# The left-over rows of the last four output tiles in one 64-row stretch at the end of a gated attention and MLP kernel

## The chip, the cores and the metric

The kernel runs on one core of one Trainium2 chip. The metric is device time in microseconds (us). A core has a matmul engine (TensorE; PE in the profile, PEld its weight loads), a vector engine (DVE), an activation engine (ACT), a general one (POOL) and SyncE (SP), from whose queue most transfers are issued. A finished tile is evicted, that is scaled and copied out of TensorE's accumulators by ACT or DVE, and then stored by a transfer to memory; a store lands when the signal of its completion arrives.

A ratio compares two kernels that ran in the same rounds, with a 95% interval; it is not quite the ratio of the medians quoted beside it. A "gain" without a view named is always a difference of such times; positions inside a run come from the trace of one profiled execution.

## The reference, cut to what matters

```python
x = A_x                                            # 2048 x 512
g = sigmoid((x * gate_w).sum(-1, keepdims=True))
a = attention(x, ...)                              # o @ wo, o: 2048 x 512
b = einsum('bsf,fd->bsd', z1 * (w_sp @ z2 + b_sp), w_out)   # u = z1 * (...): 2048 x 688
return g * a + (1 - g) * b
```

The output has 16 tiles of 128 rows. A tile is `oT.T @ wo + uT.T @ w_out`, scaled: four matmuls of 128 contraction rows for the attention part, and 688 = 5 * 128 + 48 rows for u. These 48 left-over rows are what the change is about.

## The kernel before

u of a tile is kept in 768 columns, padded with 80 zeros, and is transposed in six blocks of 128 rows. In even tiles the 48 left-over rows are the first ones of block 5 (in partitions 0 to 63, the lower half), in odd tiles the last ones of block 0 (in partitions 64 to 127, the upper half). So the left-over matmul of an even and of an odd tile each use one half of TensorE's rows, and can run side by side. The weights `w_rem` hold both halves, with zeros between, so a matmul over all 128 rows gives the same result.

```python
def ba_spat(acc, tt, start, c0=0, c1=D):          # five matmuls of 128 rows
    ...
def ba_rem(acc, tt, rows, stop, c0=0, c1=D):      # the 48 left-over rows
    nc.tensor.matmul(
        acc, lhsT=uTs[tt][rows, 5 * (1 - tt % 2), :], rhs=w_rem[rows, c0:c1], start=False, stop=stop)

def ba_tile(tt, cuts=(0, D)):                     # tiles 14 and 15
    for h, (c0, c1) in enumerate(zip(cuts, cuts[1:])):
        acc = acc_tile()[:, 0:c1 - c0]
        ba_spat(acc, tt, True, c0, c1)
        ba_rem(acc, tt, slice(0, P), False, c0, c1)       # all 128 rows
        ba_attn(acc, tt, False, True, c0, c1)
        ba_store(acc, tt, c0, c1, h > 0)                  # second piece: DVE and SP, else ACT

def ba_step(tt):                                  # tiles 0 to 13
    group = next(g for g in BA_GROUPS if tt in g)
    accs[tt] = acc_tile()
    ba_attn(accs[tt][:, :], tt, True, False)
    ba_spat(accs[tt][:, :], tt, False)
    if tt == group[-1]:
        for t in group:
            ba_rem(accs[t][:, :], t, halves[t % 2], True)  # 64 rows each, side by side
        if tt + 2 < NT - 1:
            attn_tile_64(tt + 2)                           # more 64-row work
        for t in group:
            ba_store(accs[t][:, :], t, 0, D, False)        # ACT evicts and issues

BA_GROUPS = [range(0, 4), range(4, 8), range(8, 12), range(12, 14)]
...
    ba_tile(14)
    ba_tile(15, cuts=(0, 384, D))
```

The softmax here doesn't subtract the row's maximum and nothing guards it: scores larger than these inputs give would overflow.

## Time and profile before

| | before |
|---|---|
| median, 3 runs (range) | 207.25 us (206.95 to 207.43) |
| span of the profiled run | 205.4 us |
| PE busy, of the span | 201.2 us, 98% |
| chain that ended last, on PE | 96% |

The first two lines are from the page of the kernel before: busy time of each engine with its share of the span and its instructions, and the chain that ended last by engine. The chain is followed back from the last instruction to what released each step.

```profile
PE 201.2 (98%) x1564; PEld 120.3 (59%) x1564; DVE 129.8 (63%) x282; ACT 75.4 (37%) x123; POOL 46.4 (23%) x77
...
PE 96%; DMA 2%; ACTq 0%; DVE 0%; issue 0%
```

TensorE is the bound nearly everywhere. So time is to be saved by taking work from TensorE, or behind its last matmul.

Next comes the chain of the kernel before in order of time, near its end. The columns are start and length in us, then engine, output and line. L520 is the spatial part (`uT.T @ w_out`), L514 the attention part, L524 the left-over rows.

```profile
196.69 1.08 PE mm L520 x5
197.77 0.32 PE mm L524 x2
198.09 1.19 PE mm L520 x5
199.28 0.22 PE mm L524
199.50 0.86 PE mm L514 x4
200.36 0.81 PE mm L520 x5
201.17 0.16 PE mm L524
201.33 0.65 PE mm L514 x4
201.98 0.28 PE mm L520 x5
202.26 0.06 PE mm L524
202.32 0.24 PE mm L514 x4
```

The chain gives prices directly. Five spatial matmuls of 512 columns take 1.08, so one takes 0.22. A left-over matmul over 128 rows costs the same as any other of its width: 0.22 for tile 14, 0.16 and 0.06 for the two pieces of tile 15. The 64-row pair of tiles 12 and 13 takes 0.32 for both, and the five spatial matmuls behind it take 1.19 instead of 1.08. The earlier stretches of four take 0.54, so one more pair adds 0.22. So the pair itself costs 0.22, and by difference entering the 64-row form costs about 0.10 and leaving it 0.11.

Behind the last matmul lies a tail. These are the timeline's lines of the kernel before for the two pieces of tile 15: start, length, engine, line, operation. ACTq and SPq are the issues of the two stores.

```profile
202.02 0.58 ACT L535 ACTIVATE ob<-mm,g_inv 128x384 bf16<-128x384 f32 x1 [0.89 <-PE mm L514]
202.58 0.35 DVE L531 TENSOR_SCALAR ob<-mm,g_inv 128x128 bf16<-128x128 f32 x1 [5.34 <-PE mm L514]
202.63 0.34 ACTq L536 DMA_DIRECT2D out_dram<-ob  x1
202.96 0.38 SPq L533 DMA_DIRECT2D out_dram<-ob  x1
```

The first piece is evicted by ACT and stored from its queue, the second by DVE and stored from SP. The trace has the landings at 204.28 and 204.46, and the program ends at 205.38.

### The profile page before, as it was taken

How to read it: one execution, taken by the hardware profiler on the slowest of the kernel's cores; microseconds unless marked ns; L12 is line 12 of the kernel's file. 1: busy time of each engine (PE TensorE's matmuls, PEld its weight loads, DVE VectorE, ACT ScalarE, POOL GpSimd, SP SyncE). 2: the span in 40 equal slices, each digit the busy share in tenths (PEclk: the TensorE clock that was granted, in tenths of full speed). 3: DMA queues.
4: the chain of work that ended last, by engine and by line, in shares of the span. 5: the costliest groups of instructions: out<-in, count | busy, mean ns of one | idle time of the engine just before them, and what ended most of it. 6: DMA issues, size and time to landing. Idle time of an engine off the chain costs nothing.

```text
span 205.4 us, 4012 instructions
## 1 busy us (share of the span) xinstructions
PE 201.2 (98%) x1564; PEld 120.3 (59%) x1564; DVE 129.8 (63%) x282; ACT 75.4 (37%) x123; POOL 46.4 (23%) x77
## 2 busy tenths in 40 slices
PE   8999999999999999999999999999999999999994
PEld 4566666655665555656565666555555555665642
DVE  4377575747977687979797788555566645633330
ACT  3466577796222233332424042222251136002222
POOL 5020202020522425334242442222204220200000
PEclk9999999999999999999999999999999999999999
DMA  6998599999999017940433229763566568552942
GB/s 175 265 183 186 92 212 209 206 259 206 265 245 217 3 38 158 307 91 13 83 29 63 51 38 117 143 117 71 100 161 51 119 114 181 67 97 55 145 89 78
DMA packets 90100, 27.22 MB, mean 133 GB/s; under 512 B 84225, under 2 KB 90081, under 8 KB 90081
## 3 DMA queue, kind: packets, MB, share of 16 engines
q1 hardware_dynamic: 87312, 24.55, 64.1%
q10 hardware_dynamic: 2736, 2.42, 4.3%
q8 instruction: 12, 0.20, 0.4%
q14 instruction: 8, 0.06, 0.1%
q0 software_dynamic: 32, 0.00, 0.0%
HBM read 4.15 MB, written 2.10 MB: 30 GB/s over the span
## 4 chain that ended last, share of the span: by engine, by line
PE 96%; DMA 2%; ACTq 0%; DVE 0%; issue 0%
PE mm L459 36%; PE zp L192 18%; PE mm L360 14%; PE mm L520 8%; PE mm L514 7%; PE mm L400 7%; DMA w_z<-in_B_w_in_dram 2%; PE kvacc L416 2%; PE at L472 2%; PE mm L524 1%; PE zp L312 0%; PE at L483 0%; PE zp L231 0%; ACTq L118 0%; ACTq L121 0%; PE pq L312 0%
## 5 line engine op out<-in xcount | busy, mean ns | idle before, releaser
L459 PE MATMUL mm<-z2all,wspT 128*128 128x344 bf16 x512 | 79.9, 309 | 0.0
L459 PEld LDWEIGHTS <-wspT 128*128 128x128 bf16 x512 | 49.0, 98 | 25.3
L192 PE MATMUL zp<-w_z,xT 128*128 128x344 bf16 x252 | 37.9, 309 | 0.1
L364 ACT ACTIVATE eq<-mm 128x512 bf16<-128x512 f32 x32 | 17.4, 594 | 51.4 <-PE mm L360 25.7
L368 DVE TENSOR_REDUCE zs<-eq 128x64 f32<-128x1024 bf16 x16 | 19.5, 1220 | 20.1 <-ACT eq L364 20.1
L192 PEld LDWEIGHTS <-xT 128*128 128x128 bf16 x252 | 24.3, 98 | 12.0 <-DVE xT L291 0.3
L364 ACT ACTIVATE ek<-mm 128x512 bf16<-128x512 f32 x32 | 17.3, 601 | 27.1 <-PE mm L360 27.1
L377 POOL TENSOR_TENSOR eq<-eq,ratio 128x512 bf16<-128x512 bf16 x16 | 16.9, 1056 | 44.6 <-DVE ratio L376 36.7
L464 DVE SCALAR_TENSOR_TENSOR ucat<-mm,bT,z1all 128x344 bf16<-128x344 f32 x32 | 17.4, 544 | 14.9 <-PE mm L459 14.9
L535 ACT ACTIVATE ob<-mm,g_inv 128x512 bf16<-128x512 f32 (+1 forms) x16 | 10.9, 680 | 32.4 <-PE mm L524 26.6
L368 DVE TENSOR_REDUCE zs<-ek 128x64 f32<-128x1024 bf16 x16 | 19.3, 1209 | 2.8 <-ACT ek L364 2.8
L520 PE MATMUL mm<-wspT,uT 128*128 128x512 bf16 (+2 forms) x85 | 20.1, 367 | 0.0
L360 PEld LDWEIGHTS <-xT 128*128 128x128 bf16 x128 | 12.2, 98 | 12.0
L377 POOL TENSOR_TENSOR ek<-ek,ratio 128x512 bf16<-128x512 bf16 x16 | 16.9, 1056 | 2.2 <-DVE ratio L376 1.7
L514 PE MATMUL mm<-wspT,oT 128*128 128x512 bf16 (+2 forms) x68 | 16.6, 366 | 0.0
L360 PE MATMUL mm<-wq_p,xT 128*128 128x512 bf16 x64 | 16.4, 379 | 0.0
L400 PE MATMUL mm<-wv_sb,xT 128*128 128x512 bf16 x64 | 16.4, 379 | 0.0
L360 PE MATMUL mm<-wk_p,xT 128*128 128x512 bf16 x64 | 16.3, 379 | 0.0
L210 DVE BATCH_NORM_STATS2 bn<-z2all 128x6 f32<-128x344 bf16 x32 | 14.9, 503 | 0.0
L207 ACT ACTIVATE z2all<-zp 128x688 bf16<-128x688 f32 x16 | 11.8, 743 | 7.8 <-PE zp L192 7.7
L265 ACT ACTIVATE z1all<-zp 128x688 bf16<-128x688 f32 x16 | 11.9, 743 | 5.1 <-PE zp L192 4.7
L520 PEld LDWEIGHTS <-uT 128*128 128x128 bf16 x85 | 8.1, 98 | 9.4 <-issue 0.2
(78 smaller groups left out, 145.3 us busy)
## 6 DMA issues: line engine op xcount, KB each, us to landing
out_dram<-ob ACTq DMA_DIRECT2D x15, 128.0 KB, 2.2
wspT<-in_B_w_out_dram SPq DMA_DIRECT2D x2, 640.0 KB, 5.0
w_z<-in_B_w_in_dram SPq DMA_DIRECT2D x2, 344.0 KB, 4.8
wv_sb<-in_A_wqkv_dram SPq DMA_DIRECT2D x2, 256.0 KB, 3.6
wspT<-in_A_wo_dram SPq DMA_DIRECT2D x2, 256.0 KB, 4.0
w_z<-in_B_w_in_dram SPq DMA_DIRECT2D x2, 172.0 KB, 4.2
xs<-in_A_x_dram SPq DMA_DIRECT2D x2, 128.0 KB, 2.7
uT<-ucat SPq DMA_TRANSPOSE x16, 2.8
```

What stands on the lines that cost most here:

```text
L192: nc.tensor.matmul(zp[:, j, 0:n], lhsT=xT[:, dt, tt * P:(tt + 1) * P], rhs=wt[:, dt, j * HF:j * HF + n], start=(dt == first), stop=(dt == ...
L210: nc.vector.bn_stats(out=bn6[:, tt, j, :], in_=z2v[:, j, :])
L265: nc.scalar.activation(out=z1all[:, tt, :].rearrange("p (j n) -> p j n", j=2), in_=zp[:, :, 0:HF], func=AF.Gelu_apprx_tanh,)
L360: nc.tensor.matmul(ps[:, :], lhsT=xT[:, dt, tt * P:(tt + 1) * P], rhs=w[:, dt, :], start=(dt == 0), stop=(dt == NDT - 1))
L364: nc.scalar.activation(out=e[:, :, a, :], in_=ps[:, :].rearrange("p (h f) -> p h f", f=DH), func=AF.Exp, scale=1.0 - 2.0 * a)
L368: nc.vector.tensor_reduce(out=z[:].rearrange("p h a -> p (h a)"), in_=e[:].rearrange("p h a f -> p (h a) f"), axis=AX.X, op=ALU.add,)
L377: nc.gpsimd.tensor_tensor(out=e[:, :, 1, :], in0=e[:, :, 1, :], in1=ratio[:, :, None].to_broadcast([P, H, DH]), op=ALU.mult)
L400: nc.tensor.matmul(v_ps[:, :], lhsT=xT[:, dt, tt * P:(tt + 1) * P], rhs=wv_sb[:, dt, :], start=(dt == 0), stop=(dt == NDT - 1))
L459: nc.tensor.matmul(gp[:, 0:HF], lhsT=wspT[:, st, tt * P:(tt + 1) * P], rhs=z2all[:, st, j * HF:(j + 1) * HF], start=(st == 0), stop=(st == ...
L464: nc.vector.scalar_tensor_tensor(out=ucat[tt % NU][:, c0 + j * HF:c0 + (j + 1) * HF], in0=gp[:, 0:HF], scalar=bT[:, tt:tt + 1], in1=z1all[ ...
L514: nc.tensor.matmul(acc, lhsT=oTs[tt][:, g, :], rhs=wo_t[:, g, c0:c1], start=start and g == 0, stop=stop and g == NG - 1)
L520: nc.tensor.matmul(acc, lhsT=uTs[tt][:, i + ft, :], rhs=w_main[i][:, ft, c0:c1], start=start and ft == 0, stop=False)
```

## The change

Its intent: tile 14's left-over matmul (lower half) should run beside those of tile 15's two pieces (upper half), in the 64-row stretch that tiles 12 and 13 pay for anyway. As tiles 12 to 14 are then evicted late, DVE takes one of them, and SP issues all three stores so that ACT is free for tile 15. The core of the diff:

```diff
-    def ba_rem(acc, tt, rows, stop, c0=0, c1=D):
+    def ba_rem(acc, tt, start=False, c0=0, c1=D):
+        rows = halves[tt % 2]
         nc.tensor.matmul(
-            acc, lhsT=uTs[tt][rows, 5 * (1 - tt % 2), :], rhs=w_rem[rows, c0:c1], start=False, stop=stop)
+            acc, lhsT=uTs[tt][rows, 5 * (1 - tt % 2), :], rhs=w_rem[rows, c0:c1], start=start, stop=not start)
 ...
-            nc.scalar.dma_start(out=dst, in_=ob[:, :])
+            (nc.sync if on_sp else nc.scalar).dma_start(out=dst, in_=ob[:, :])
 ...
-    def ba_tile(tt, cuts=(0, D)):
 ...
+    def ba_last():
+        last = NT - 1
+        ba_step(last - 1)
+        pieces = [(acc_tile()[:, 0:384], 0, 384), (bank_tile(q_bank)[:, 0:P], 384, D)]
+        for t in BA_GROUPS[-1][:-1]:
+            ba_rem(accs[t][:, :], t)
+        for acc, c0, c1 in pieces:
+            ba_rem(acc, last, True, c0, c1)
+        for n, t in enumerate(BA_GROUPS[-1][:-1]):
+            ba_store(accs[t][:, :], t, on_dve=n == 1, on_sp=True)
+        for n, (acc, c0, c1) in enumerate(pieces):
+            ba_spat(acc, last, False, c0, c1)
+            ba_attn(acc, last, False, True, c0, c1)
+            ba_store(acc, last, c0, c1, on_dve=n == 1)
 ...
-    BA_GROUPS = [range(0, 4), range(4, 8), range(8, 12), range(12, 14)]
+    BA_GROUPS = [range(0, 4), range(4, 8), range(8, 12), range(12, 16)]
 ...
-        ba_tile(14)
-        ba_tile(15, cuts=(0, 384, D))
+        ba_last()
```

More of the change, by code (lines that the diff above doesn't have):

```diff
@@ L521, in ba_spat, with ba_store @@
                              start=start and ft == 0, stop=False)
-    def ba_rem(acc, tt, rows, stop, c0=0, c1=D):
+    def ba_rem(acc, tt, start=False, c0=0, c1=D):
+        rows = halves[tt % 2]
         nc.tensor.matmul(
-            acc, lhsT=uTs[tt][rows, 5 * (1 - tt % 2), :], rhs=w_rem[rows, c0:c1], start=False, stop=stop)
-    def ba_store(acc, tt, c0, c1, on_dve):
+            acc, lhsT=uTs[tt][rows, 5 * (1 - tt % 2), :], rhs=w_rem[rows, c0:c1], start=start, stop=not start)
+    def ba_store(acc, tt, c0=0, c1=D, on_dve=False, on_sp=False):
         ob = work.tile([P, c1 - c0], BF16, name=f"ob{c1 - c0}", bufs=4 if c1 - c0 == D else 1)
@@ L540, in acc_tile @@
         return bank_tile(acc_banks[-1])
-    def ba_tile(tt, cuts=(0, D)):
-        for h, (c0, c1) in enumerate(zip(cuts, cuts[1:])):
-            acc = acc_tile()[:, 0:c1 - c0]
-            ba_spat(acc, tt, True, c0, c1)
-            ba_rem(acc, tt, slice(0, P), False, c0, c1)
-            ba_attn(acc, tt, False, True, c0, c1)
-            ba_store(acc, tt, c0, c1, h > 0)
+    def ba_last():
[12 more added lines that the diff above has]
+            ba_store(acc, last, c0, c1, on_dve=n == 1)
     def ba_step(tt):
@@ L556, in ba_step @@
             for t in group:
-                ba_rem(accs[t][:, :], t, halves[t % 2], True)
-            if tt + 2 < NT - 1:
-                attn_tile_64(tt + 2)
+                ba_rem(accs[t][:, :], t)
+            attn_tile_64(tt + 2)
             for t in group:
-                ba_store(accs[t][:, :], t, 0, D, False)
+                ba_store(accs[t][:, :], t)
     oTs = {}
```

## The prediction

> **What bounds the kernel now.** TensorE. The page's busy table gives PE 201.2 us of a span of 205.4 us (98%) at a full granted clock, and the chain that ended last is PE for 96%. So the change is worth what it takes from TensorE's last 5 us, plus or minus what it does to the tail behind it.
>
> **What the change does to TensorE.** Matmul counts and weight loads stay (3130 PE rows in both, the same up to tile 13's spatial matmuls). In the chain of waits, in time order from 197.77 us (end of tile 13's spatial part), before has: 64-row pair of tiles 12 and 13 0.32, tile 14 1.19 + 0.22 + 0.86, first piece of 15 0.81 + 0.16 + 0.65, second piece 0.28 + 0.06 + 0.24, end at 202.56. Costs to read from it:
> - 128-row left-over matmuls: 0.22 (512 columns), 0.16 (384), 0.06 (128), together 0.44 us;
> - the 64-row pair costs 0.22 for both, as they run side by side, plus about 0.10 on entry (0.32 less 0.22) and 0.11 on leaving (the next five spatial matmuls take 1.19 instead of 1.08). The Trainium skill ("TensorEngine Tiling (Array Packing)", Key Properties) says changing the tiling mode drains TensorE and that different tiles run in parallel; this trace agrees with both. The stretch of four at 187.87 takes 0.54, one more pair for 0.22.
>
> After, the stretch holds tiles 12, 13, 14 and both pieces of 15. Tile 14 (lower rows, 512 columns) runs beside 384 + 128 columns of tile 15 (upper rows), so it should cost 0.54. Entry and exit stay one each. Estimate from these durations: 0.86 + 1.08 (tile 14), 0.54, then 0.92 + 0.65 and 0.28 + 0.24 = 4.57, so the last matmul ends near 202.34 instead of 202.56: 0.22 us less, all on the chain.
>
> **Inputs in time?** Tile 14 now starts with attention, needed at 197.6; its transposed o landed near 195.6. Tile 15's transposed u landed near 199.0 and is now needed near 199.9, not 200.2. Its o landed near 200.0, needed near 201.0. Slack about 0.9 us; no new wait.
>
> **Stores.** Tiles 12, 13 and 14 are evacuated only after the stretch, near 200.05: 12 and 14 on ACT (0.69 each), 13 on DVE (128 columns take 0.35; estimate for 512 about 0.75), all three issued from SP (0.38 each), done by about 202.0. All are free for the pieces, at 201.8 and 202.35. The stores start about 0.4 us apart and should land by 203.5 (1.7 us each before). The last DVE eviction, issue and landing (0.35 + 1.5 us) then keep their length and shift by 0.22 us.
>
> **Predicted time:** 207.25 - 0.22 = 207.0 us, range 206.75 to 207.3 (before: 206.95 to 207.43). Chances: faster by over 2% 0.01, within 2% 0.98, slower 0.01.
>
> **What would show it right.** The chain has one 64-row group of five of about 0.54 us, no 128-row left-over matmul, and the last matmul ends about 0.22 us earlier; the last store is issued about 0.22 us earlier with the same 1.5 us to landing.
>
> **What would make it wrong.** A PE wait for tile 15's u before the stretch; the two pieces of 15 not running beside tile 14 (stretch 0.7 or more); an ACT, DVE or SP still busy with tiles 12 to 14 when tile 15's pieces end; the three bunched stores delaying the last landing.

## The result, and the profile after

| | before | after |
|---|---|---|
| median, 6 runs each (range) | 207.34 us (206.93 to 207.74) | 207.05 us (206.99 to 207.24) |
| ratio | 1 | 0.999, 95% interval 0.9975 to 1.0005 |
| span of the profiled run | 205.4 us | 205.3 us |

The times alone cannot tell the change from nothing: the interval contains 1. The trace can. This is the chain after, from the same point (the end of tile 13's spatial part); L525 is the left-over rows, L532 the last eviction.

```profile
196.80 1.08 PE mm L520 x5
197.88 0.86 PE mm L514 x4
198.74 1.08 PE mm L520 x5
199.82 0.54 PE mm L525 x4
200.36 0.92 PE mm L520 x5
201.28 0.65 PE mm L514 x4
201.93 0.28 PE mm L520 x5
202.21 0.24 PE mm L514 x4
202.44 0.02 issue
202.47 0.35 DVE ob L532
```

The three left-over matmuls on 128 rows are gone, and one stretch of 0.54 holds all five (the chain counts four; one that runs beside another is not a link of it). From the end of tile 13's spatial part to the end of the last matmul it is 202.44 - 197.88 = 4.56 us; before it was 202.56 - 197.77 = 4.79. (The chain follows the last matmul to its signal, 0.01 to 0.02 later than the matmul's own end, which the table below uses.)

The timeline's lines of the tail after, beginning with the last of the three stores that SP issues for tiles 12 to 14:

```profile
201.83 0.40 SPq L537 DMA_DIRECT2D out_dram<-ob  x1
201.96 0.58 ACT L536 ACTIVATE ob<-mm,g_inv 128x384 bf16<-128x384 f32 x1 [0.52 <-PE mm L514]
202.47 0.35 DVE L532 TENSOR_SCALAR ob<-mm,g_inv 128x128 bf16<-128x128 f32 x1 [1.45 <-PE mm L514]
202.57 0.34 ACTq L537 DMA_DIRECT2D out_dram<-ob  x1
202.85 0.33 SPq L534 DMA_DIRECT2D out_dram<-ob  x1
```

All engines are free in time for tile 15. But the two last issues are now 0.27 us apart (before 0.33), and the last store took 1.57 us to land (before 1.50). So of TensorE's 0.22 us, about 0.15 reach the last landing.

Why the times are so blurred can also be read from the traces. In every trace whose kernel is unchanged up to there, 150.84 to 150.87 us pass from the first matmul with `w_sp` (L459, which makes u) to the end of tile 13's spatial part. That first matmul itself, however, starts anywhere from 46.43 to 47.32 us; in all but one (e2) the difference is already there at 9 us, among the first loads and matmuls. These 0.9 us are about as wide as the spread of the times, several times the effect, and come before anything that the change touches. So the experiments are read in two ways: by their times where some tenths of a per cent are expected, and else by distances inside a trace, from the end of tile 13's spatial part.

This table is worked out from the traces, in us, in the order: end of tile 13's spatial part to the last matmul's own end; distance of the two last store issues; time to landing of the first and of the second piece of tile 15; end of tile 13's spatial part to the last landing. The labels are those of the experiments below.

```
                     to last matmul  issues apart  first lands  second lands  to last landing
before                   4.770          0.329         1.650        1.499          6.688
after                    4.553          0.271         1.669        1.565          6.535
e8 (after again)         4.553          0.273         1.656        1.550          6.521
e1 (order)               4.557          0.272         1.656        1.550          6.524
e9 (order, widths)       4.557          0.272         1.669        1.564          6.539
e2 (two stretches)       4.768          0.272         1.654        1.549          6.734
e3 (all on 128 rows)     4.773          0.272         1.667        1.561          6.751
e5 (15 on 128 rows)      4.767          0.328         1.653        1.491          6.675
e4 (all on ACT)          4.552       first is last    1.628        1.487          7.953
e6 (two issues on ACT)   4.553       first is last    1.628        1.506          6.798
e7 (cut at 416)          4.553          0.092         1.740        1.814          6.751
e10 (cut at 368)         4.554          0.362         1.661        1.505          6.493
e11 (cut at 352)         4.553          0.450         1.650        1.513          6.516
```

### The profile page after: what moved, and what is told of

The parts are those of the page before. It is cut to its first block, busy times and chain, and to the rows that moved or that the text cites. A ratio compares the mean times of both kernels' runs of the same rounds, so it can differ in the third digit from the quotient of the medians.

```text
span 205.3 us, 4014 instructions
## 1 busy us (share of the span) xinstructions
PE 201.2 (98%) x1564; PEld 120.2 (59%) x1564; DVE 130.5 (64%) x283; ACT 74.6 (36%) x122; POOL 46.4 (23%) x77
## 4 chain that ended last, share of the span: by engine, by line
PE 95%; DMA 2%; ACTq 0%; DVE 0%; issue 0%
PE mm L459 36%; PE zp L192 18%; PE mm L360 14%; PE mm L520 8%; PE mm L514 7%; PE mm L400 7%; DMA w_z<-in_B_w_in_dram 2%; PE kvacc L416 2%; PE at L472 2%; PE mm L525 1%; PE zp L312 0%; PE at L483 0%; PE zp L231 0%; ACTq L118 0%; ACTq L121 0%; PE pq L312 0%
## 5 line engine op out<-in xcount | busy, mean ns | idle before, releaser
L459 PE MATMUL mm<-z2all,wspT 128*128 128x344 bf16 x512 | 79.9, 309 | 0.0
L459 PEld LDWEIGHTS <-wspT 128*128 128x128 bf16 x512 | 49.0, 98 | 25.3
L536 ACT ACTIVATE ob<-mm,g_inv 128x512 bf16<-128x512 f32 (+1 forms) x15 | 10.1, 680 | 33.1 <-PE mm L525 28.5
```

The lines of the kernel that those rows point to most:

```text
L459: nc.tensor.matmul(gp[:, 0:HF], lhsT=wspT[:, st, tt * P:(tt + 1) * P], rhs=z2all[:, st, j * HF:(j + 1) * HF], start=(st == 0), stop=(st == ...
```

## The experiments

The theory: tile 14's left-over matmul takes no time of its own because it runs beside those of tile 15, and this is the whole gain on TensorE. Rivals: a 64-row matmul is cheaper as such; one stretch instead of several forms saves the switch; the moved evictions and stores are the gain. All kernels below are edits of the changed kernel, and all gave correct results.

### e5_last_full: tile 14 in the stretch, tile 15 not

```diff
-        for acc, c0, c1 in pieces:
-            ba_rem(acc, last, True, c0, c1)
 ...
-            ba_spat(acc, last, False, c0, c1)
+            ba_spat(acc, last, True, c0, c1)
+            nc.tensor.matmul(acc, lhsT=uTs[last][:, 0, :], rhs=w_rem[:, c0:c1], start=False, stop=False)
```

> The changed kernel's stores and one stretch, but only tiles 12, 13 and 14 in it; the two pieces of 15 take their left-over rows on all 128 rows, as before. Theory (pairing 14 with 15 is the whole gain): 14 stands alone in its turn, so tile 13's spatial end to the last matmul's end is 4.79 us as before, ratio to before 1.000. Rival (moved stores, or tile 14 as 64 rows, are the gain): 4.6 us or less, or a span as short as the changed kernel's.

Ratio to before 0.9999 (0.9982 to 1.0017), median 207.1 beside 207.18. The chain of this run, with L553 the left-over rows of tile 15 on 128 rows:

```profile
199.88 0.53 PE mm L525 x3
200.41 0.92 PE mm L520 x5
201.33 0.16 PE mm L553
...
202.42 0.06 PE mm L553
```

The stretch with three matmuls takes 0.53, no less than the one with five after the change (0.54), and the 0.16 and 0.06 of tile 15 are back on top. To the last matmul it is 4.77 us, as before. A 64-row matmul alone is therefore not cheaper, and stores and evictions moved as in the change bring nothing to TensorE. The gain is the pairing.

### e2_two_stretches: the pairing kept, the one stretch undone

```diff
-    BA_GROUPS = [range(0, 4), range(4, 8), range(8, 12), range(12, 16)]
+    BA_GROUPS = [range(0, 4), range(4, 8), range(8, 12), range(12, 14), range(14, 16)]
 ...
-            attn_tile_64(tt + 2)
+            if tt + 2 < NT - 1:
+                attn_tile_64(tt + 2)
 ...
-            ba_store(accs[t][:, :], t, on_dve=n == 1, on_sp=True)
+            ba_store(accs[t][:, :], t)
```

> Tiles 12 and 13 have their own 64-row stretch with stores on ACT as before; 14 and the two pieces of 15 share a second one. The pairing of 14 with 15 is kept, and one more entry and exit is paid. Theory (pairing is worth 0.22, one entry and exit 0.10 + 0.11): from tile 13's spatial end to the last matmul's end 4.76 us, within 0.03 of before's 4.79; so no gain without the one stretch. Rival (the switch costs nothing once the pipe is full): 4.56 us, as the changed kernel. Ratio to before 0.999 to 1.000.

Ratio 1.001 (0.9989 to 1.003), median 207.29 beside 207.03. Its chain:

```profile
197.91 0.32 PE mm L525 x2
198.23 0.97 PE mm L514 x4
199.20 1.08 PE mm L520 x5
200.28 0.33 PE mm L525 x2
200.61 0.92 PE mm L520 x5
```

Both pairs cost 0.32 to 0.33, and behind both the next group is longer by 0.11 (0.97 for 0.86, 0.92 for 0.81). The second entry and exit eat the 0.22 that the pairing saves: 4.77 us to the last matmul. Collecting all five in one stretch is a needed half of the change.

### e3_full_rows: every pairing undone

```diff
-        rows = halves[tt % 2]
+        rows = slice(0, P)
```

> The changed kernel with all 17 left-over matmuls on all 128 rows (same result, the other rows meet zeros): every pairing is undone, in the three earlier groups too. Theory (each pair hides 0.216 us, all of it on the chain): each earlier group's four take about 0.43 us more (two pairs), 1.30 in all; the last group is as in the kernel before. So 1.3 us longer than before, ratio 1.006. Rival (TensorE's spare time hides it, or the 64-row form and the switches eat what pairing gives): ratio 1.000 to 1.002.

Median 208.68 beside 207.03, ratio 1.0079 (1.0059 to 1.0099), so slower clear of noise; the mean is longer by 1.6 us, with an interval of about 1.2 to 2.0, so 1.3 is inside it. The left-over group of the third of the earlier stretches and the attention matmuls behind it, in the chain of the kernel before and then in the chain of this run (the groups of the other two stretches take 0.54 and 0.86 as well):

```profile
187.87 0.54 PE mm L524 x4
188.41 0.19 PE at L483 x16
```

```profile
188.88 0.86 PE mm L525 x4
189.75 0.30 PE at L483 x16
```

Four matmuls take 0.86 instead of 0.54, and the entry into the 64-row form, about 0.1, is then paid by the attention matmuls behind them (L483, 0.30 instead of 0.19). From the first matmul at L459 to the end of tile 13's spatial part it is 152.13 us instead of 150.84: 1.29, as expected. The pairing's price list holds at six times the size and shows in the times.

### e1_order and e9_widths: does the order in the stretch matter?

```diff
-        for t in BA_GROUPS[-1][:-1]:
+        for t in (12, 14, 13):
```

> Same instructions as the changed kernel, but the stretch runs 12, 14, 13, 15, 15: tiles 12 and 14 lie in the lower rows, 13 and both pieces of 15 in the upper ones, so 14 no longer runs beside 15. Theory (the gain is the pairing of 14 with 15): the five-matmul group in the chain of waits takes about 0.76 us instead of 0.54, tile 13's spatial end to the last matmul's end is about 4.78 us (4.56 after, 4.79 before), the gain is gone, ratio to before 1.000. Rival 1 (a 64-row matmul is cheaper as such): order does not matter, group stays at 0.54, 4.56 us. Rival 2 (the moved stores are the gain): the stores' engines are as in the changed kernel, so the gain stays.

This expectation missed. The median was 206.7 beside 207.03, ratio 0.9991 (0.9971 to 1.0011), the chain's group took 0.54, and it is 4.56 us to the last matmul: the gain stayed. Either the order in the program is not the order of execution, or the theory of pairing is wrong. In this run the matmuls of 12, 13 and 14 cannot be told apart by width, so a second order was tried in which they can:

```diff
-        for t in BA_GROUPS[-1][:-1]:
+        for t in (12, 14):
             ba_rem(accs[t][:, :], t)
         for acc, c0, c1 in pieces:
             ba_rem(acc, last, True, c0, c1)
+        ba_rem(accs[13][:, :], 13)
```

> Follows up the miss of the run that swapped 13 and 14: there the group still took 0.54 us, so TensorE may have run 13 ahead of 14. Here the stretch's order in the program is 12 (512 columns, lower rows), 14 (512, lower), 15 (384, upper), 15 (128, upper), 13 (512, upper), so the widths tell who runs beside whom. If a matmul on the free row half overtakes one that waits for the busy half: the first 64x384 starts within 10 ns of the first 64x512, the group takes 0.54 to 0.55 us. If matmuls start strictly in program order: the 64x384 starts 0.22 us after the first 64x512, with 14, and the group takes about 0.76 us.

The compiled program keeps the order 512 (tile 12), 512 (14), 384 and 128 (15), 512 (13). The profile has, for the left-over line between 200.03 and 200.21 us, the matmuls' count, shortest, median and longest length in ns, first and last start in us, and forms:

```profile
L525 PE MATMUL mm<-wspT,uT x2: 332/359/386, 200.0 to 200.0; 64*128 64x512 bf16 x1, 64*128 64x384 bf16 x1
```

A 512-column and the 384-column matmul start together: the trace has 200.039 and 200.045. The next start is the 128-column one at 200.218, then the other two of 512 at 200.264 and 200.274. So the 384-column matmul, third in the program, overtook the second, which started only when the row half that the first kept busy came free. The group took 0.54. TensorE itself found the partners. In e1's trace, too, two 512-column matmuls start 0.007 us apart, at 199.370 and 199.377, and the third starts with the 384-column one 0.22 us later: e1 had not undone the pairing at all, and its miss does not speak against it. Whether the completion signals keep the program's order when matmuls overtake one another is not shown here; in these runs ACT was busy with tile 12 and came to tile 14 well after the stretch, and the results were right.

### e4_stores_act: evictions and issues of 12 to 14 all on ACT

```diff
-            ba_store(accs[t][:, :], t, on_dve=n == 1, on_sp=True)
+            ba_store(accs[t][:, :], t)
```

> The changed kernel with tiles 12, 13 and 14 evicted on ACT and issued from ACT, as before the change. TensorE as in the changed kernel (4.56 us to the last matmul). Theory (moving evictions to DVE and issues to SP is what lets the gain through): an eviction and issue on ACT take 1.16 us from start to start, so the first piece of 15 is evicted from about 203.65 instead of 201.96 and lands about 1.5 us later than the last landing does now; 1.5 us longer than the changed kernel, ratio to before 1.006. Rival (the stores are off the chain): no change, ratio 0.999.

Median 208.3 beside 207.03, ratio 1.0061 (1.0041 to 1.0081). TensorE is as in the changed kernel (4.55), but the end of this run's chain is ACT:

```profile
201.88 0.70 ACT ob L536
202.58 0.02 issue
202.60 0.34 ACTq L537
202.94 0.05 issue
202.99 0.58 ACT ob L536
```

The last landing is 1.42 us later than in the changed kernel (7.95 against 6.53; 1.5 was expected). So the moved stores give nothing by themselves, but without them the late evictions would cost over six times what the pairing saves.

### e6_issue_act: issues on ACT, tile 13's eviction on DVE

```diff
-            ba_store(accs[t][:, :], t, on_dve=n == 1, on_sp=True)
+            ba_store(accs[t][:, :], t, on_dve=n == 1)
```

> The changed kernel with tile 13 evicted on DVE as there, but the three stores issued from ACT instead of SP. TensorE as in the changed kernel. Theory: ACT now does two evictions (0.69 each) and three issues (0.34 and a gap) before the first piece of 15, which it starts near 202.8 instead of 201.96; it lands near 205.1 instead of 204.24, which makes it the last landing (204.41 in the changed kernel): about 0.65 us longer, ratio to the kernel before 1.002. Rival: off the chain, ratio 0.999.

The expectation misread the edit: an eviction on DVE is always stored from SP, so only two of the three issues moved to ACT. ACT came to the first piece of tile 15 4.56 us after the end of tile 13's spatial part instead of 4.09. The first piece's store was then the last to land, and the end came 0.26 us later than in the changed kernel (6.80 against 6.53), not 0.65. Median 207.44 beside 207.18, ratio 1.0015 (0.9999 to 1.0032): the interval just contains 1, the direction agrees, and the expected size was wrong.

### e8_after_again: the changed kernel once more

No edit.

> The changed kernel once more, unchanged, in five rounds. Theory: 4.56 us from tile 13's spatial end to the last matmul, exactly as in the first trace; last store 1.50 to 1.57 us to landing; ratio to before 0.999, a gain of 0.15 to 0.23 us. If the longer last landing of the first trace (1.565 against 1.499 before) is due to the bunched stores it comes again; if it is chance it does not.

Median 206.84 beside 207.18, ratio 0.999 (0.9973 to 1.0008), the same value as in the first rounds, and again with 1 inside the interval. In the trace TensorE's stretch is equal to the nanosecond (4.553), and the last landing again took 1.55 us: the longer landing is not chance.

### e7_split_416, e10_split_368, e11_split_352: what holds the last landing

Each is a change of one cut, here that of e10 (e7 has 416 and 96 columns, e11 352 and 160):

```diff
-        pieces = [(acc_tile()[:, 0:384], 0, 384), (bank_tile(q_bank)[:, 0:P], 384, D)]
+        pieces = [(acc_tile()[:, 0:368], 0, 368), (bank_tile(q_bank)[:, 0:144], 368, D)]
```

> The changed kernel with the last tile cut at 416 instead of 384 columns: a shorter last eviction (estimate 0.22 + 0.00104 a column: 0.32 instead of 0.35 us) against a first piece whose last matmul is 0.12 us nearer to the end. TensorE's total is the same. Theory: the two landings come within 0.05 us of one another and the end moves by no more than 0.04 us; not to be seen in the times, ratio 0.999. Rival (the first piece becomes the last to land): its landing is the later by 0.05 or more and the span grows.

e7: median 207.3 beside 207.18, ratio 1.0009 (0.9991 to 1.0027). (The estimate for the eviction is a line through DVE's 0.35 us for 128 columns and 0.75 for 512 in the trace after the change; the 96 columns took 0.32.) Neither expectation was right: the end moved by more than 0.04 us, but not because the first piece became the last to land. It still landed 0.17 us before the second. The first piece's matmuls end later, so the two issues come 0.09 us apart, both stores take longer (1.74 and 1.81 us), and the end is 0.22 us later than in the changed kernel (6.75 against 6.53), which is as much as TensorE had saved. Its timeline's lines of the two issues:

```profile
202.78 0.37 ACTq L537 DMA_DIRECT2D out_dram<-ob  x1
202.87 0.33 SPq L534 DMA_DIRECT2D out_dram<-ob  x1
```

> The changed kernel with the last tile cut at 368 instead of 384 columns. Theory from the runs so far: the last landing is held by the first piece's store when the two issues are less than about 0.33 us apart (0.27 now, last landing 1.55 to 1.57 us; 0.33 in the kernel before and in the run with the pieces on 128 rows, 1.49 to 1.50). The first piece is ready about 0.07 us earlier, the second's eviction is 0.02 longer, so the issues are 0.36 apart, the last landing takes 1.49, and from tile 13's spatial end to the last landing it takes 6.48 us (6.53 and 6.52 in the two traces of the changed kernel, 6.69 before). Rival (the three bunched stores of 12 to 14 lengthen it): 1.55 stays and the end is 0.02 later. Times: ratio 0.9985 to 0.999.

> The same with the cut at 352: issues about 0.45 us apart, last landing 1.49 us, the second eviction 0.03 longer than at 384: 6.50 us from tile 13's spatial end to the last landing. So the best cut is near 368, and the whole difference between 352 and 384 stays below 0.06 us, not to be seen in the times.

e10: median 207.01 beside 207.15, ratio 0.9996 (0.9982 to 1.0009). e11: 206.99 beside 207.15, ratio 0.9996 (0.9982 to 1.0011). The issues of e10 in its timeline:

```profile
202.59 0.34 ACTq L537 DMA_DIRECT2D out_dram<-ob  x1
202.95 0.33 SPq L534 DMA_DIRECT2D out_dram<-ob  x1
```

They are 0.36 us apart, the last landing takes 1.51 us, and the last landing comes at 6.49 us, 0.03 to 0.04 earlier than in the two traces of the changed kernel (6.52 and 6.53); e11 gains at most 0.02. By the trace, 368 is the best of the four cuts, but on one trace each, and two traces of the same kernel already differ by 0.014. The times do not confirm it, and cannot at this size.

The rival for the longer landing, the three bunched stores of tiles 12 to 14, is refuted by runs on both sides. e5 has them bunched and its last store lands in 1.49 us, with the issues 0.33 apart; e2 has them spread out and its last store takes 1.55, with the issues 0.27 apart. What goes with a long landing is the distance of the last two issues. The Trainium skill ("Trainium Kernel Development and Optimization", Key Constraints) says that transfers issued from the SP and ACT queues run on the same 16 DMA engines and interleave. The landings are tied to one another: where the issues are 0.27 us apart or closer and SP's store is the last, it lands 0.166 to 0.167 us after the first, whatever its own issue time (e5, at 0.328, has 0.166 too). But the packets of SP's queue in the traces put little of the delay into the moving of data. From its issue to its last data packet the second store took 1.148 us before, 1.165 after and 1.150 in e8; from that packet to the landing it took 0.351 before and 0.400 in both traces of the changed kernel. So most of what was added lies behind the data, and sharing the engines explains at best a part of it. What holds the signal there is open.

## Why the prediction was right

- **TensorE bounds the end, and the change saves 0.22 us there.** Right. The sum predicted from the prices of the kernel before (0.86 + 1.08 + 0.54 + 0.92 + 0.65 + 0.28 + 0.24) is term by term what the chain after shows: 4.57 us expected, 4.56 measured. The Trainium skill ("TensorEngine Tiling (Array Packing)", Key Properties) names both sides of it, the drain at a change of form and the parallel tiles; the runs put 0.10 + 0.11 us and a whole matmul on them (e2, e5, e3).
- **The cause is the pairing of tile 14 with tile 15.** Right, by e5 (without it the gain is gone) and e3 (all pairings undone cost 1.3 us more in the earlier groups alone). The one stretch is needed as well (e2).
- **Inputs in time, no new wait.** Right: tile 15's transposed u landed at 199.08, and its left-over matmul started at 199.98. No idle time of TensorE appears in the chain.
- **The stores of tiles 12 to 14 do not delay tile 15.** Right: SP was done at 202.23 and tile 15's store was issued at 202.85, though the last of the three stores landed at 203.62 and not by 203.5. e4 shows that this was bought by DVE and SP.
- **"The last DVE eviction, issue and landing ... keep their length and shift by 0.22 us."** This is the one term that was mis-sized. Eviction and issue kept theirs. The landing grew from 1.50 to 1.57 and 1.55 us, so that the last landing moved by 0.15 and 0.17 us. The second piece's left-over matmul used to lie between the two pieces' ends; with it gone, the first piece gained only 0.16 us and the second 0.22, the two stores came 0.06 us closer, and the last one landed later after its issue. That the distance of the issues goes with it is shown by e5, e2 and e7; how the first store holds up the second is not.
- **207.0 us, within 2%.** Right: 207.05. But that the figure fits so closely is partly luck: the spread of the runs is wider than the gain, and a change that did nothing could have landed inside the predicted 206.75 to 207.3 as well (the kernel before had 207.25 when it was predicted). The times show 0.999 twice with intervals that contain 1. e1, e10 and e11, which also end earlier by the trace, lie below 1 too (0.9991, 0.9996, 0.9996), none of them clear of noise. So that the change makes the kernel faster is known from the distances in the trace, not from the times.

## What to carry to other kernels

In this kernel a matmul that uses half of TensorE's rows cost a whole matmul when alone (e5: 0.53 us for a pair and one more) and nothing beside a partner on the other half (0.54 for all five), but entering and leaving the form cost together 0.21 us, about as much as one 512-column matmul: collect enough pairs in one place. At the end of a program, look at what the last two stores do to each other before counting a gain on the compute engine in full. When an effect is smaller than the spread of the times, find a point in the trace from which every run is alike, and measure from there.

## What the Trainium skill lacked or had wrong

- "TensorE: Matmul & The Clock Gate" (Part 3, The mechanism) says that matmuls start and end strictly in program order; "PSUM — Partial Sum Buffer" (Engine vs sequencer instructions) says the same. In e9 a 64-row matmul of 384 columns, third in the program, started 6 ns after the first and about 0.22 us before the second, which needed the busy row half.
- "TensorEngine Tiling (Array Packing)" (Key Properties) says that changing the tiling mode drains TensorE, without a price. Here it is about 0.10 us on entry and 0.11 on leaving (0.32 for a pair that takes 0.22, and 1.19 for five matmuls that take 1.08).
- The pages say that transfers of different queues interleave on the same engines, but none was found that gives how much later a small store lands behind another. Here a 32 KB store took 1.49 to 1.50 us to land when issued 0.33 us after a 96 KB one and 1.55 to 1.57 at 0.27; a 36 KB store took 1.51 at 0.36 after one of 92 KB, and a 24 KB one 1.81 at 0.09 after one of 104 KB.
